# Mask comparisons as differences on GpSimd and signs on ScalarE, rounded query rows copied by a transfer, and reciprocals one unit behind their addition

## The chip, the cores and the metric

One core of one Trainium2 chip runs the kernel. The metric is the device time of one execution in microseconds. Before the change three runs gave a median of 675.91 us (671.8 to 677.35).

## What is computed

The reference is clustered attention followed by two feed-forward blocks, all in float32:

```
# attention: B=2, H=8, S=768, D=64, 16 clusters for each head
q_assign = argmax(normalised q . normalised centroids)      # one of 16 for each query
k_assign = argmax(normalised k . normalised centroids)
mask     = q_assign[..., :, None] == k_assign[..., None, :]
scores   = where(mask, q @ k.T / sqrt(D), -1e9)
attn     = softmax(scores) @ v
# first block: 1536 tokens, 512 -> 2048 -> 512, a rational function between the products
# second block: 512 -> 1024 -> 512, h * softmax(h), a layer norm, then the product
```

The first of equal maxima counts in the argmax.

## The kernel before

**Attention units.** A unit is one head n (16 of them, two batches of 8) and one tile t of 128 queries (6 of them): 96 units. `unit_scores` (L384, L390) makes 128x768 scores in PSUM with four products; there are two such PSUM buffers. Queries and keys are split into rounded parts and remainders, so that the products run in the faster float format: `q1` holds rounded q in rows 0 to 63 and the remainder of q in rows 64 to 127, `q2` holds rounded q again in rows 0 to 63 and 16 rows of the cluster mask behind them; `k1` and `k2` likewise. `unit_max` takes the minimum of the negated scores on VectorE (L395), `unit_exp` the exponential on ScalarE (L408), which also sums a row into `rs`. For every second unit `turn_p` transposes the exponentials on VectorE (L425), and `pv_step` multiplies them with v on TensorE (L435) one head later.

**Heads.** `prep_head(n + 1)` runs in seven steps beside the units of head n, on GpSimd: it rounds k (through `rnd`, L339), takes the remainder of k (L353), rounds q into `q1` and `q2` (both L339), takes the remainder of q (L358) and starts the transfers of the 16 mask rows (L362, L363) on SP's queue. `load_head` (L193, L194) and `load_v` (L202) load later heads on the same queue.

**Masks.** Heads are assigned in five sets. Sets 2, 3 and 4 (two pairs of heads each, q and k) run beside the units, from units 8, 27 and 50; `TCH` says for each step how many units behind that it is placed. `two_sims` and `keep` bring the similarities to the centroids, `to_token` transposes them on VectorE (L302), `top` takes the maximum of each group of 16 (L306), `is_top` compares with it (L310), `rank` multiplies the hits with 16, 15, ..., 1 on GpSimd (L285), `top` and `is_top` again leave only the first hit, `from_token` transposes back (L313), and `mask_out` (L320) scales the result to 0 or a huge number for q and 0 or 1 for k.

**Sums.** For each pair of heads `pair_sums` adds a tiny number to the sums on ScalarE (L460) and takes the reciprocal on VectorE (L461), in the unit t = 0 of the next even head; `sums_out` transposes them two units later on TensorE (L475), sends them through DRAM (L481, L484), and `pair_fin` multiplies with them on GpSimd (L496, L510).

**Order.** The framework orders each engine's instructions by when they are ready in its own model of the program, earlier code first among those that are ready; an engine then runs its queue in that order. `issue_after` and `behind` put an instruction behind another in the queue of its engine. The steps of the masks are queued behind the minimum of their unit on VectorE. Weight conversions for the first block (`w1_f32`: L135 and L138 on ScalarE, L142 on VectorE; `to_parts`: L146, L147) are spread over units 28 to 94. Behind attention come the first block (`ff_h` L745, `ff_y` L797) and the second (`t_h` L873, `t_out` L924).

Of the kernel before, what the change touches and what calls it, by code (L numbers as in the profile page):

```python
# [7 lines left out]
F32 = mybir.dt.float32  # L8
F32R = mybir.dt.float32r
BF16 = mybir.dt.bfloat16  # L10
AF = mybir.ActivationFunctionType
# [5 lines left out]
C = 16  # L17
# [13 lines left out]
def fused_kernel(ctx: ExitStack, tc: tile.TileContext, qT, kT, v, cent, w1, w2i, w2o, gln, coef, centT, cst, out):  # L31
# [20 lines left out]
    def psum1(name):  # L52
# [14 lines left out]
    identb = const.tile([128, 128], BF16, name="identb")  # L67
    nc.gpsimd.tensor_copy(identb, ident)
    rev = cst_t[:, 128:128 + C]
    big = const.tile([128, 1], F32, name="big")  # L70
    nc.vector.memset(big, BIG)
    less = const.tile([128, 1], F32, name="less")
# [17 lines left out]
    S1B = 2  # L90
    AT = (0, 0, 8, 27, 50)
    TCH = {
# [3 lines left out]
    }  # L96

    OLAG = 2
# [141 lines left out]
    def scales(k):  # L240
        es = sets[k]
        m = sm.tile([128, 3], F32, name=f"msc{k}", tag="msc", bufs=2)
        for j, (pp, i) in enumerate(es):
            nc.gpsimd.memset(m[32 * j:32 * j + 32, 0:1], 1.0 if i else -BIG)
            nc.gpsimd.memset(m[32 * j:32 * j + 32, 1:2], 0.0 if i else BIG)
            p = pp % 4
            (nc.vector if k < 1 else nc.gpsimd).tensor_copy(m[32 * j:32 * j + 32, 2:3], cnr[32 * p:32 * p + 32])
        OH[k] = qk.tile([128, S], F32R, name=f"oh{k}", tag="oh", bufs=2)
        for j, (pp, i) in enumerate(es):
            for h in range(2):  # L250
                mk[2 * pp + h, i] = OH[k][32 * j + 16 * h:32 * j + 16 * h + 16]
        MS[k] = m
# [29 lines left out]
    def rank(k, eng):  # L282
        g = 2 * len(sets[k]) * NT
        ev = E[k][1].rearrange("p t (g c) -> p (t g) c", c=C)
        eng.tensor_tensor(ev, ev, rev[:, None, :].to_broadcast([128, g, C]), op=ALU.mult)  # L285
# [19 lines left out]
        tops[k] = sm.tile([128, 48], F32, name=f"my{k}", tag="my48", bufs=2)  # L305
        nc.vector.tensor_reduce(tops[k], E[k][1].rearrange("p t (g c) -> p (t g) c", c=C), axis=AX.X, op=ALU.max)  # L306

    def is_top(k):
        ev = E[k][1].rearrange("p t (g c) -> p (t g) c", c=C)
        nc.vector.tensor_tensor(ev, ev, tops[k][:, :, None].to_broadcast([128, 48, C]), op=ALU.is_equal)  # L310

    def from_token(k):
        nc.vector.transpose(E[k][0], E[k][1].rearrange("p t c -> p (t c)"))  # L313
# [3 lines left out]
    def mask_out(k, o, t):  # L317
        masked[k] += o.shape[-1] * (o.shape[1] if len(o.shape) > 2 else 1)
        M = t.shape[0]
        nc.scalar.activation(out=o, in_=t, func=AF.Identity, scale=MS[k][0:M, 0:1], bias=MS[k][0:M, 1:2])  # L320
# [13 lines left out]
    def rnd(eng, o, a, scale=1.0):  # L334
        if eng is nc.scalar:
            eng.activation(out=o, in_=a, func=AF.Copy, scale=scale)
            return
        if eng is nc.gpsimd:
            eng.tensor_scalar(o, a, scale, 0.0, op0=ALU.mult, op1=ALU.add)  # L339
        elif isinstance(scale, float) and scale == 1.0:  # L340
            eng.tensor_copy(o, a)
        else:
            eng.tensor_scalar(o, a, scale, None, op0=ALU.mult)

    def prep_head(n, er=None, es=None):
        er = er or nc.gpsimd
        es = es or nc.gpsimd
        b, h = divmod(n, H)
        i = n % NB
        a, c = raw.pop(("d", n, 0)), raw.pop(("d", n, 1))  # L350
        rnd(er, k1[i], c, sgn[:, 1:2])
        yield
        es.tensor_tensor(k2[i][0:64], c[0:64], k1[i][0:64].bitcast(F32), op=ALU.subtract)  # L353
        yield
        rnd(er, q1[i], a, sgn[:, 0:1])
        rnd(er, q2[i][0:64], a[0:64], -0.125)
        yield
        es.tensor_tensor(q1[i][64:128], a[64:128], q1[i][64:128].bitcast(F32), op=ALU.subtract)  # L358
        yield
        if n:  # L360
            assert masked[next(k for k, es in enumerate(sets) if (n // 2, 0) in es)] == S
            nc.sync.dma_start(out=q2[i][64:80].bitcast(F32), in_=mk.pop((n, 0)).bitcast(F32))  # L362
            nc.sync.dma_start(out=k2[i][64:80].bitcast(F32), in_=mk.pop((n, 1)).bitcast(F32))  # L363
        yield
# [92 lines left out]
    def pair_sums(key):  # L457

        r = rs.pop(key)
        nc.scalar.activation(out=r, in_=r, func=AF.Identity, bias=tiny)  # L460
        nc.vector.reciprocal(r, r)  # L461
        if key < 7:
            return r

        rw = fin.tile([128, S], F32, name="rw", tag="rb", bufs=1)
        nc.vector.tensor_copy(rw.rearrange("p (t j d) -> p j t d", t=NT, j=2), r[:, :, :, None].to_broadcast([128, 2, NT, D]))
        rb = psum2("s", "rbp")
        for t in range(NT):
            nc.tensor.transpose(rb[:, t // 3, t % 3 * 128:t % 3 * 128 + 128], rw[:, t * 128:t * 128 + 128], ident)
        rsd[key] = rb  # L470

    def sums_out(key, r, u):

        def turned(sp):
            return nc.tensor.transpose(sp[0:12, 0, 384:512], r.rearrange("p j t -> p (j t)"), ident)  # L475

        def spread_out(sp):
            rt = sm.tile([12, 128], F32, name=f"rt{key}", tag="rt", bufs=2)
            nc.scalar.activation(out=rt, in_=sp[0:12, 0, 384:512], func=AF.Copy)
            d = dram.tile([2, S], F32, name=f"rd{key}", tag="rd")  # L480
            nc.sync.dma_start(out=d.rearrange("j (t p) -> (j t) p", p=128), in_=rt)  # L481
            rb = fin.tile([128, S], F32, name=f"rb{key}", tag="rb", bufs=1)
            for j in range(2):
                nc.sync.dma_start(out=rb[64 * j:64 * j + 64], in_=d[j:j + 1, :].to_broadcast([64, S]))  # L484
            rsd[key] = rb

        while u in pre:
            u += 1
        pre[u], post_ = [turned], post.setdefault(u, [])
        post_.append(spread_out)  # L490
# [45 lines left out]
    def assign(k, u, tch):  # L536

        def hook(d, u, f):
            d.setdefault(u, []).append(f)

        def two_sims(c):
            def g(sp):
                for t in range(2):
                    r = sims(k, 2 * c + t, 1, sp[:, t, 384:512])
                return r
            return g

        hook(post, u + tch[0], lambda sp: scales(k))
        for c in range(3):
            hook(pre, u + tch[c], two_sims(c))  # L550
            hook(post, u + tch[c], lambda sp, c=c: keep(k, 2 * c, 2, sp[:, :, 384:512]))
        steps = (to_token, top, is_top, lambda k: rank(k, nc.gpsimd), top, is_top, from_token, lambda k: mask_out(k, OH[k], E[k][0]))
        for i, f in enumerate(steps):
            hook(post, u + tch[3 + i], lambda sp, f=f: f(k))

# [80 lines left out]
    def pv_part(n, t):  # L636
# [4 lines left out]
            return n - 1, c[t - 3], c[t - 2]  # L641
        return (n - 2, (7, 10)[t], (10, 12)[t]) if t < 2 else (-1, 0, 0)

    units = [(n, t) for n in range(B * H) for t in range(NT)]
    NS = S // 64
    for idx, (n, t) in enumerate(units):
# [21 lines left out]
        if m_ >= 0:  # L668
            for i in range(i0, i1):
                pv_step(m_, i)  # L670
        if t == 0 and n and n % 2 == 0:
            sums_out(n // 2 - 1, pair_sums(n // 2 - 1), idx + 2)
        unit_exp(n, t, sp, m)
        if n >= 2 and t in (1, 2):
            pv_out(n - 2, t - 1)
# [345 lines left out]
```

## Time and profile before

| | before |
|---|---|
| median of 3 runs | 675.91 us |
| the profiled execution | 673.62 us |
| its span, first to last instruction | 671.8 us |
| mean granted TensorE clock, share of 2.4 GHz | 0.972 |
| TensorE products busy | 609.3 us (91%) |
| VectorE busy | 495.5 us (74%) |
| ScalarE busy | 437.6 us (65%) |
| GpSimd busy | 391.6 us (58%) |
| moved by DMA | 64.71 MB |

PE is TensorE's products and PEld its weight loads, DVE is VectorE, ACT ScalarE, POOL GpSimd and SP the engine that issues most transfers. A busy share is an average over stages with different limits. Attention fills the span up to about 235 us, the first block follows up to about 500 us, the second to the end.

### The profile page before, as it was taken

To read this page: it belongs to the slowest core of one execution; us is meant where nothing else is said; L and a number is where in the kernel's file an instruction comes from. 1 tells how busy PE (TensorE), PEld (TensorE's weight loads), DVE (VectorE), ACT (ScalarE), POOL (GpSimd) and SP (SyncE) were. 2 spreads that over 40 slices of the span, in tenths; PEclk is the share of its full clock that TensorE was granted. 3 is DMA by queue.
4 is the path that set the end of the run, shared out by engine and by line. 5 is a ranking of instruction groups with operands and counts; after the bars stand their busy time and mean duration, and the time that the engine had idled before them with its cause. 6 is when DMAs were issued, how large, how long until landed. Compare 5 with 4: busy or idle time off the path is not lost.

```text
span 671.8 us, 13803 instructions
## 1 busy us (share of the span) xinstructions
PE 609.3 (91%) x5517; PEld 471.8 (70%) x5517; DVE 495.5 (74%) x648; ACT 437.6 (65%) x796; POOL 391.6 (58%) x363
## 2 busy tenths in 40 slices
PE   7697978888878768999999999999998999999998
PEld 3465655555555556788788777788886888888887
DVE  4789999999999738888977588867689464544360
ACT  2456656765787649989878898786676344434341
POOL 7455667656889338999869899976788000000000
PEclk8589899998999989999999999999998999999999
DMA  8955687777663222323103433300100000000001
GB/s 226 272 180 159 151 224 179 186 193 187 168 182 95 56 96 94 126 95 125 64 0 112 134 111 116 93 1 0 33 0 1 0 1 32 16 32 16 32 17 47
DMA packets 22439, 64.71 MB, mean 96 GB/s; under 512 B 4532, under 2 KB 5640, under 8 KB 22376
## 3 DMA queue, kind: packets, MB, share of 16 engines
q1 hardware_dynamic: 21944, 63.67, 33.4%
q8 instruction: 43, 0.70, 0.4%
q10 hardware_dynamic: 432, 0.17, 0.1%
q14 instruction: 20, 0.16, 0.1%
HBM read 59.16 MB, written 3.19 MB: 93 GB/s over the span
## 4 chain that ended last, share of the span: by engine, by line
PE 42%; POOL 8%; ACT 6%; DVE 3%; issue 2%; DMA 2%; ACTq 0%; POOLq 0%; DVEq 0%
PE y L797 11%; PE hh L873 10%; PE o L924 10%; PE h L745 10%; POOL q L761 2%; POOL gl L780 2%; PE lt L906 2%; POOL q L760 1%; DMA rawv<-in_w2i 1%; POOL vl L147 1%; POOL w1l L147 1%; ACT t L758 1%; ACT h L769 1%; ACT y L759 1%; DVE w1w L142 1%
## 5 line engine op out<-in xcount | busy, mean ns | idle before, releaser
L745 PE MATMUL h<-xhl,w1h 128*128 128x512 f32 x384 | 121.8, 393 | 5.0 <-DVE y L774 3.2
L408 ACT ACTIVATE p<-s,m 128x768 f32<-128x768 f32 x96 | 86.0, 897 | 58.1 <-DVE m L395 57.9
L395 DVE TENSOR_REDUCE m<-s 128x1 f32<-128x768 f32 x96 | 88.4, 933 | 15.8 <-PE s L390 15.4
L435 PE MATMUL pv<-pt,v 32*64 32x192 f32 x3072 | 84.3, 338 | 9.7 <-ACT w L451 6.1
L745 PEld LDWEIGHTS h<-xhl,w1h 128*128 128x128 f32 x384 | 71.7, 188 | 22.5 <-DVE y L774 4.7
L425 DVE STREAM_TRANSPOSE pt<-p 128x1536 f32<-128x1536 f32 x48 | 84.4, 1761 | 0.0
L384 PE MATMUL s<-k,q 128*128 128x384 f32 x192 | 62.5, 410 | 21.9 <-ACT p L408 21.1
L797 PE MATMUL y<-gl,w1h 128*128 128x512 f32 x192 | 76.5, 398 | 5.7 <-POOL gl L780 5.7
L435 PEld LDWEIGHTS pv<-pt,v 32*64 32x64 f32 x3072 | 57.2, 134 | 30.5 <-issue 16.1
L797 PE MATMUL y<-gh,w1l 128*128 128x512 f32 x192 | 76.1, 396 | 0.0
L745 PE MATMUL h<-xhl,w1l 128*128 128x512 f32 x192 | 75.4, 393 | 0.0
L780 POOL TENSOR_TENSOR gl<-y,gh 128x512 fp32r<-128x512 f32 x48 | 66.4, 1384 | 11.5 <-ACT gh L779 11.4
L797 PE MATMUL y<-gh,w1h 128*128 128x512 f32 x192 | 69.6, 394 | 0.1
L761 POOL TENSOR_TENSOR q<-q,t 128x512 f32<-128x512 f32 x48 | 65.3, 1360 | 3.1
L384 PEld LDWEIGHTS s<-k,q 128*128 128x128 f32 x192 | 31.1, 202 | 49.3 <-ACT p L408 27.7
L760 POOL TENSOR_SCALAR q<-t,ab 128x512 f32<-128x512 f32 x48 | 41.9, 873 | 29.7 <-ACT t L758 20.3
L762 DVE TENSOR_TENSOR y<-y,h 128x512 f32<-128x512 f32 x48 | 32.8, 683 | 32.3 <-ACT y L759 32.1
L390 PE MATMUL s<-k,q 128*128 128x384 f32 x192 | 52.4, 356 | 2.3 <-DVE k L595 2.3
L873 PE MATMUL hh<-vh,xhl 128*128 128x512 f32 x192 | 53.9, 395 | 0.0
L797 PEld LDWEIGHTS y<-gl,w1h 128*128 128x128 f32 x192 | 36.3, 189 | 17.0 <-POOL gl L780 9.1
L797 PEld LDWEIGHTS y<-gh,w1h 128*128 128x128 f32 x192 | 36.1, 189 | 8.6 <-ACT gh L779 0.5
L797 PEld LDWEIGHTS y<-gh,w1l 128*128 128x128 f32 x192 | 36.3, 189 | 8.0
(151 smaller groups left out, 1330.5 us busy)
## 6 DMA issues: line engine op xcount, KB each, us to landing
raww<-in_w SPq DMA_DIRECT2D x32, 512.0 KB, 4.5
v<-in_v SPq DMA_DIRECT2D x64, 192.0 KB, 4.6
dup<-in_qT SPq DMA_DIRECT2D x31, 192.0 KB, 4.1
dup<-in_kT SPq DMA_DIRECT2D x31, 192.0 KB, 3.8
rawv<-in_w2i SPq DMA_DIRECT2D x8, 512.0 KB, 3.5
rawv<-in_w2o SPq DMA_DIRECT2D x8, 512.0 KB, 3.5
out<-ob SPq DMA_DIRECT2D x11, 256.0 KB, 2.0
pr<-in_qT SPq DMA_DIRECT2D x7, 384.0 KB, 4.0
```

Of the source, the lines that this page charges most:

```text
L384: r = nc.tensor.matmul(sp[:, a, 0:384], lhsT=q1[i][:, sl], rhs=k1[i][:, a * 384:(a + 1) * 384], start=True, stop=False)
L390: last["pe"] = nc.tensor.matmul(sp[:, a, 0:384], lhsT=q2[i][:, sl], rhs=k2[i][:, a * 384:(a + 1) * 384], start=False, stop=True)
L395: last["dve"] = nc.vector.tensor_reduce(m, sp[:, :, 0:384], axis=AX.XY, op=ALU.min)
L408: last["act"] = nc.scalar.activation(out=P[n, t // 2][:, t % 2], in_=sp[:, :, 0:384], func=AF.Exp, scale=-1.0, bias=m, accum_out=rs[key][: ...
L425: r = nc.vector.transpose(PT[n][:, 2 * i:2 * i + 2].rearrange("p t k -> p (t k)"), p.rearrange("p t a k -> p (t a k)"))
L435: last["pv"] = nc.tensor.matmul(pv[n][64 * c:64 * c + 64, r, 0:192].rearrange("p (t q) -> p t q", t=NT), lhsT=vv[n][sl, j], rhs=PT[n][sl, ...
L745: r = nc.tensor.matmul(hp, lhsT=w[:, kt * 128:(kt + 1) * 128], rhs=x[:, kt], start=(i == 0), stop=(i == 11))
L761: nc.gpsimd.tensor_tensor(q, q, t, op=ALU.mult)
L780: nc.gpsimd.tensor_tensor(gl, y, gh.bitcast(F32), op=ALU.subtract)
L797: nc.tensor.matmul(o, lhsT=w[:, c], rhs=g, start=(first and i == 0), stop=(last and i == 2))
L873: last["th"] = nc.tensor.matmul(hp[:, a], lhsT=y[:, kt], rhs=w[:, 512 * a:512 * a + 512], start=(kt == 0 and e == 0), stop=(kt == 3 and e ...
L924: r = nc.tensor.matmul(op[:, 0:m], lhsT=l[:, kt], rhs=w, start=(n == 0), stop=(n == 23))
```

## The change

In sets 2, 3 and 4 the two comparisons become a difference to the maximum on GpSimd (`below`) and its sign on ScalarE (`hot`): 0 at the maximum, -1 elsewhere. The rank step becomes an addition of 16/32, 15/32, ... on GpSimd (`rank_at`), after which only the first hit is the maximum. `mask_out` has another offset to fit. Two steps are added, so `TCH` is written anew; the second maximum comes earlier in it than before. In `prep_head` rows 0 to 63 of `q2` are no longer rounded on GpSimd but copied from `q1` by a transfer on SP's queue. `sums_out` is called one unit later than `pair_sums`, and the reciprocal of the first seven pairs moves into it, queued on VectorE behind the minimum of that unit.

```
+    rev_n = const.tile([128, C], F32, name="revn")
+    nc.vector.tensor_scalar(rev_n, rev, 2.0 ** -5, None, op0=ALU.mult)
...
-        2: (0, 1, 2, 3, 4, 5, 6, 10, 11, 12, 13),
-        3: (0, 1, 2, 3, 5, 6, 7, 12, 13, 14, 15),
-        4: (0, 1, 2, 3, 5, 6, 7, 12, 13, 14, 15),
+        2: (0, 1, 2, 3, 4, 4, 5, 6, 9, 9, 11, 12, 13),
+        3: (0, 1, 2, 3, 5, 5, 6, 7, 10, 10, 13, 14, 15),
+        4: (0, 1, 2, 3, 5, 5, 6, 7, 10, 10, 13, 14, 15),
...
-            nc.gpsimd.memset(m[32 * j:32 * j + 32, 1:2], 0.0 if i else BIG)
+            nc.gpsimd.memset(m[32 * j:32 * j + 32, 1:2], (0.0 if i else BIG) if k < 2 else float(i))
...
-    def is_top(k):
+    def below(k):
         ev = E[k][1].rearrange("p t (g c) -> p (t g) c", c=C)
-        nc.vector.tensor_tensor(ev, ev, tops[k][:, :, None].to_broadcast([128, 48, C]), op=ALU.is_equal)
+        nc.gpsimd.tensor_tensor(ev, ev, tops[k][:, :, None].to_broadcast([128, 48, C]), op=ALU.subtract)
+
+    def rank_at(k):
+        ev = E[k][1].rearrange("p t (g c) -> p (t g) c", c=C)
+        nc.gpsimd.tensor_tensor(ev, ev, rev_n[:, None, :].to_broadcast([128, 48, C]), op=ALU.add)
+
+    def hot(k):
+        ev = E[k][1].rearrange("p t c -> p (t c)")
+        nc.scalar.activation(out=ev, in_=ev, func=AF.Sign)
...
         rnd(er, q1[i], a, sgn[:, 0:1])
-        rnd(er, q2[i][0:64], a[0:64], -0.125)
+        nc.sync.dma_start(out=q2[i][0:64].bitcast(F32), in_=q1[i][0:64].bitcast(F32))
...
-        nc.vector.reciprocal(r, r)
         if key < 7:
             return r
+        nc.vector.reciprocal(r, r)
...
+        behind(nc.vector.reciprocal(r, r), last["dve"])
         while u in pre:
...
-        steps = (to_token, top, is_top, lambda k: rank(k, nc.gpsimd), top, is_top, from_token, lambda k: mask_out(k, OH[k], E[k][0]))
+        steps = (to_token, top, below, hot, rank_at, top, below, hot, from_token, lambda k: mask_out(k, OH[k], E[k][0]))
...
+    due = []
...
-        if t == 0 and n and n % 2 == 0:
-            sums_out(n // 2 - 1, pair_sums(n // 2 - 1), idx + 2)
+        if t < 2 and n and n % 2 == 0:
+            if t:
+                sums_out(n // 2 - 1, due.pop(), idx + 2)
+            else:
+                due.append(pair_sums(n // 2 - 1))
```

## Rows read from the trace of the kernel before

**Rows 1.** Busy time of engines in four stretches: span, then engines, clock, DMA.

```profile
core 0: us, PE busy (x) PEld busy (x) DVE busy (x) ACT busy (x) POOL busy (x), PEclk, DMA share, GB/s
45.00:230.00 185.00, 153.01 (x3157) 106.83 (x3161) 171.94 (x161) 128.41 (x250) 128.46 (x111) 0.98 0.64 169
250.00:500.00 250.00, 243.76 (x1049) 195.84 (x1048) 199.69 (x277) 210.17 (x355) 211.96 (x175) 1.00 0.24 76
63.00:72.00 9.00, 6.90 (x109) 4.64 (x110) 9.00 (x9) 5.85 (x11) 6.54 (x15) 0.81 0.73 181
146.00:157.00 11.00, 7.76 (x135) 5.07 (x141) 10.33 (x9) 6.11 (x13) 8.95 (x8) 0.84 0.86 219
```

**Rows 2.** Groups of instructions by form, 45 to 230 us.

```profile
line engine op names shapes xcount | busy us, mean ns | idle before us <-releasers
L395 DVE TENSOR_REDUCE m<-s 128x1 f32<-128x768 f32 x84 | 77.2, 932 | 8.0 <-PE s L390 7.6
...
L425 DVE STREAM_TRANSPOSE pt<-p 128x1536 f32<-128x1536 f32 x42 | 73.9, 1761 | 0.0
...
L339 POOL TENSOR_SCALAR q<-dup 64x768 fp32r<-64x768 f32 x13 | 11.5, 884 | 0.0
...
L142 DVE SCALAR_TENSOR_TENSOR w1f<-w1f,raww 128x512 uint32<-128x512 uint32 x10 | 9.8, 976 | 0.0
...
L310 DVE TENSOR_TENSOR e<-e,my 128x768 f32<-128x768 f32 x6 | 8.3, 1381 | 0.0
...
L285 POOL TENSOR_TENSOR e<-e,cst 128x768 f32<-128x768 f32 x3 | 5.8, 1939 | 3.7 <-DVE e L310 3.7
...
L320 ACT ACTIVATE oh<-sm,msc 128x768 fp32r<-128x768 f32 x3 | 3.0, 1016 | 0.0
```

**Rows 3.** Waits, 45 to 230 us, then SP's of the whole span: total, times, longest.

```profile
ACT p L408 <- DVE m L395: 49.5, 43, 2.6
...
PE s L384 <- ACT p L408: 17.1, 25, 1.7
...
DVE m L395 <- PE s L390: 7.6, 10, 1.3
...
DVE rs L461 <- ACT rs L460: 5.3, 5, 1.4
...
SPq L193 <- POOL k L353: 27.3, 8, 4.2
```

**Rows 4.** VectorE in order of time: start, duration, instruction, idle before.

```profile
147.57 2.22 DVE L310 TENSOR_TENSOR e<-e,my 128x768 f32<-128x768 f32 x1
149.71 0.68 DVE L142 SCALAR_TENSOR_TENSOR w1f<-w1f,raww 128x512 uint32<-128x512 uint32 x1
...
166.41 0.92 DVE L310 TENSOR_TENSOR e<-e,my 128x768 f32<-128x768 f32 x1
```

**Rows 5.** TensorE in order of time, behind the first and the sixth comparison.

```profile
52.59 0.62 PE L384 MATMUL s<-k,q 128*128 128x384 f32 x2 [0.73 <-ACT p L408]
...
169.43 0.59 PE L384 MATMUL s<-k,q 128*128 128x384 f32 x2 [1.42 <-ACT p L408]
```

**Rows 6.** VectorE and TensorE in order of time around one reciprocal.

```profile
129.61 0.23 DVE L461 RECIPROCAL rs<-rs 128x12 f32<-128x12 f32 x1 [0.82 <-ACT rs L460]
129.75 1.75 DVE L395 TENSOR_REDUCE m<-s 128x1 f32<-128x768 f32 x2
...
129.79 0.51 PE L390 MATMUL s<-k,q 128*128 128x384 f32 x2
```

**Rows 7.** GpSimd in order of time, beside the comparison at 147.57.

```profile
147.16 1.81 POOL L496 TENSOR_TENSOR u<-u,w 128x768 f32<-128x768 f32 x1 [2.05 <-ACT w L451]
```

**Rows 8.** Head 7's rounding, its first scores, and transfers with KB and landing.

```profile
102.07 0.91 POOL L339 TENSOR_SCALAR q<-dup,sgn 128x768 fp32r<-128x768 f32 x1
...
114.15 0.59 PE L384 MATMUL s<-k,q 128*128 128x384 f32 x2 [0.94 <-ACT p L408]
...
dup<-in_kT SPq DMA_DIRECT2D x31, 192.0 KB, 3.8
```

**Rows 9.** VectorE and GpSimd in order of time at the start.

```profile
5.46 0.15 DVE L226 TENSOR_SCALAR cnr<-cnr 128x1 f32<-128x1 f32 x1 [4.09 <-POOL cnr L225]
...
8.23 0.60 POOL L68 CAST identb<-cst 128x128 bf16<-128x128 f32 x1
```

## The prediction

> **What bounds the kernel now.** I read the windows first [rows 1]. From 45 to 230 us the attention units run, 84 of the 96. VectorE is busy 171.9 of 185 us there, TensorE 153.0, ScalarE 128.4 and GpSimd 128.5. From 250 to 500 us, in the feed-forward part, TensorE is busy 243.8 of 250. So attention is paced by VectorE with TensorE close behind, and the rest by TensorE. Whatever attention ends earlier, the whole kernel ends earlier, because the part behind it has nothing else to wait for.
>
> The table of groups [rows 2] says what VectorE does: the minimum of a unit (0.932 us each) and the transpose of two units (1.761 us) are 151.1 us of the 172. The reader is to see that what is left is small and that the mask comparisons (L310) are its second largest item: 6 instructions, 8.3 us, 1.381 us each.
>
> The waits [rows 3] confirm the order: the exponential on ScalarE waits 49.5 us for the minimum on VectorE, and TensorE's scores wait 17.1 us for an exponential that must free their PSUM buffer (there are two). VectorE itself waits only 7.6 us for scores and 5.3 us, 5 times, for the addition ahead of the reciprocal (L461).
>
> A unit costs 185/84 = 2.20 us. Two numbers are enough to see how tight the ring is: VectorE needs (77.2 + 73.9)/84 = 1.80 us for each unit, TensorE 153.0/84 = 1.82 us. Time that leaves VectorE comes out at the end only where TensorE then stands idle and can start earlier.
>
> **The change part by part.**
>
> **Comparisons off VectorE.** Six instructions go. They took between 0.92 us (at 166.41) and 2.22 us (at 147.57), and the next instruction starts 0.08 us before the listed end (149.71 against 147.57 + 2.22 = 149.79) [rows 4]. With that overlap for each, 8.3 - 0.5 = 7.8 us leave the queue. Does TensorE wait behind them? Behind the first it sits idle 0.73 us, behind the sixth 1.42 us, each time for an exponential, and there is such a gap of 0.7 to 1.7 us behind all six [rows 5]. So I take all of it: **-7.8**, with -3.9 as the poor end, if half of each gap only becomes a wait for scores.
>
> **TensorE's clock.** Around two of the long comparisons the granted clock was 0.81 (9 us) and 0.84 (11 us) of the 2.4 GHz level, while it was 0.98 over the stage [rows 1]: TensorE had stood idle just before. That is 9 x 0.19 + 11 x 0.16 = 3.5 us of lost clock. Some of it was idle time anyhow. I take **-1.0**, between 0 and -3.5.
>
> **Reciprocals one unit later.** The five waits of 5.3 us go [rows 3]. What is late next? At 129.61 VectorE waited 0.82 us; the two minima behind it then ran back to back from 129.75 [rows 6]. Without the wait the first could start at once. The second needs scores that TensorE finished only at 130.30 and would start there instead of at about 130.6. So of 0.82 us about 0.3 is gained directly; the first exponential, and with it the next scores, comes some 0.8 us sooner, which the transposes partly hide. 0.4 us for each of five is **-2.0**, between 0 and -5.3. The transposition of the sums on TensorE follows two units behind, so nothing waits for the moved reciprocal.
>
> **Signs on ScalarE.** Six 128x768 activations from SBUF to SBUF are added; the same form, the mask's last step (L320), takes 1.016 us [rows 2]. ScalarE has 49.5 us of waiting in 43 places [rows 3], so most fit. One that stands ahead of an exponential whose minimum is ready delays it by up to 1.0 us. Behind a minimum there is 0.93 + 1.76 = 2.7 us of VectorE work before the next-but-one minimum, while exponential and scores need some 2.1 us, so about half a us of such a delay is free. I take **+1.5** for all six, between 0 and +6.1.
>
> **Differences on GpSimd.** Six 128x768 subtractions are added; the rank multiplication becomes an addition of the same form (L285, 1.939 us) [rows 2]: 6 x 1.94 = 11.6 us more. The rounded copies of q leave: 13 in the stage of 0.884 us each = 11.5 us less. GpSimd is idle 57 us in the stage [rows 1], so its own time costs nothing. What counts is who waits for it. VectorE's second maximum now waits for a chain subtraction, sign, addition of 1.94 + 1.02 + 1.94 = 4.9 us, and its last transposition for 1.94 + 1.02 = 3.0 us. The unit numbers leave 5 units for the first chain (4 to 9, 5 to 10), some 11 us, and 3 or 4 units for the second, at least 6.6 us. Queued on VectorE behind a late one are the next minimum and hence the exponential. Between no wait and six waits of the size of the reciprocals' (5.3/5 = 1.06 us each, 6.4) I take **+1.2**, nearest to none, because of these distances.
>
> **Both engines at one port.** At 147.57 the comparison took 2.22 us, not 0.92, while a GpSimd addition ran from 147.16 to 148.97 [rows 4, 7]: VectorE's own 0.92 us began only when GpSimd had ended. The weight conversions (L142, 10 of them, 0.976 us on average against the 0.68 of the one at 149.71) remain and have two inputs in SBUF too [rows 2, 4]. GpSimd holds 11.6 us more in long pieces and 11.5 us less in short ones, so I take **+0.5**, between 0 and +5.8 (half of 1.94 us for each new piece).
> The Trainium skill's page "SBUF — State Buffer", section "Who interferes with whom", says that a VectorE instruction with two SBUF inputs and a GpSimd instruction that reads SBUF exclude each other for a whole instruction. By that rule, the trace agrees at 147.57, and the moved comparisons would come to hold against VectorE what they used to suffer.
>
> **Copies of q by transfer.** 15 transfers of 192 KB, on SP's queue, replace 15 GpSimd steps. Each waits for the rounding of q. For head 7 that ended at 102.98 and its first scores started at 114.15 [rows 8], 11.2 us later; a transfer of this size, a key half, lands in 3.8 us [rows 8], and the masks' transfers go into the same tile behind it in any case. SP already waits 27.3 us for GpSimd's key remainder ahead of the next loads [rows 3], so what is queued behind the new transfer (next head's q, k and v) is not the late one. If that cover were gone, a head would start 3.8 us late. **0**, up to +1.
>
> **A constant at the start.** One 128x16 product on VectorE, about the 0.15 us of L226; if it stands ahead of L226 and its input lands only when GpSimd reads it (8.23 us), it costs 8.23 - 5.46 = 2.8 us [rows 9]. **+0.1**, between 0 and 2.8, as it can be queued later.
>
> **The sum**: -7.8 - 1.0 - 2.0 + 1.5 + 1.2 + 0.5 + 0 + 0.1 = **-7.5 us**. The profiled execution took 673.6 us (span 671.8 and 1.8 us around it) and would take 666.1. The median of the runs shown, 675.9, lies 2.3 us above it; against that the forecast is **668.4 us**, 1.1% less.
>
> **The rivals.**
>
> *Signs hold up the exponentials (slower).* ScalarE works in order. If the sign of a unit is queued ahead of the next exponential, that one waits for the subtraction and the sign: 1.94 + 1.02 = 3.0 us behind the maximum, while its own minimum is ready 0.9 us behind it, so 2.1 us late; 4.0 us if GpSimd first ends another long product. Six times 3.0 is 18 us against the 10.8 gained: +7.2, about **683**. It decides from 1.8 us a piece (10.8/6). For it: sets 3 and 4 give the first sign one unit, 2.2 us, less than these 3.0. Against it: a queue's order is not the code's. GpSimd ran the second remainder for head 3 ahead of set 2's rank step, which comes earlier in the code and was not ready; a sign may be put behind an exponential in the same way.
>
> *TensorE takes over.* At 1.82 us a unit it needs as much as VectorE. Half of the comparisons (-3.9), 0.3 us for each reciprocal (-1.5), costs as above (+3.3): -2.1, about **674**. For it: the minima waited for scores 10 times even now. Against it: TensorE's idle gaps stand just behind the comparisons.
>
> *Everything comes through.* -7.8 - 3.5 - 5.3 and no more than 1.6 of costs: -15, **661**.
>
> *The port.* The forecast plus the bound of the port, 5.3 us more: **674**. This is what the skill's rule above would do if each new piece met a VectorE instruction with two inputs; there are only 10 such, and their mean of 0.976 us says that a few are met now.
>
> **How the numbers follow.** Chances: forecast 0.52, signs 0.12, TensorE 0.22, everything 0.10, port 0.04. Under 1%, about 6.8 us, this kernel's measurement hardly tells from no change. The forecast lies at that edge, on its far side in some 7 of 10 of its cases. Faster by over 1%: 0.10 + 0.36 + 0.03 = 0.49; within: 0.39; slower: 0.12. The range runs from 660 (everything) to 678 (the milder half of the signs' case) and leaves out 2 in 10.
>
> **What would show it.** Right: no L310 on VectorE, its busy time in the stage some 8 to 10 us less, no wait of VectorE for the addition of the sums, the windows at 63 and 146 us at clock 0.95 or more, feed-forward starting 7 us earlier. Wrong: ScalarE waiting for GpSimd ahead of a sign, VectorE waiting for GpSimd ahead of the second maximum, TensorE's scores waiting for the transfer of q, or the minima waiting for scores by as much as the comparisons cost.

## The result and the profile after

The changed kernel takes 683.29 us (median of 4 runs, 680.84 to 687.6) against 675.47 us for the kernel before: ratio 1.0123, 95% interval 1.0081 to 1.0165. The forecast was 668.4 us with a range up to 678. The time is that of the rival in which signs hold up the exponentials, which gave 683 us and had a chance of 0.12.

The profiled execution took 687.6 us (before: 673.62). It is the slowest of the four, 4.3 us above the median, so its waits are read for their kind and place more than for their sum. Lines have moved in the changed kernel: scores are L394 and L400, the minimum L405, the exponential L418; of the masks' steps, the maximum is L308, the difference L312, the rank addition L316 and the sign L320.

The windows come first (columns as in [rows 1]):

```profile
core 0: us, PE busy (x) PEld busy (x) DVE busy (x) ACT busy (x) POOL busy (x), PEclk, DMA share, GB/s
45.00:230.00 185.00, 148.95 (x2927) 104.43 (x2918) 152.55 (x146) 123.71 (x239) 119.45 (x99) 0.92 0.68 177
250.00:500.00 250.00, 239.46 (x1197) 193.11 (x1198) 189.79 (x265) 202.74 (x344) 206.15 (x168) 0.99 0.25 81
100.00:120.00 20.00, 9.02 (x173) 6.22 (x157) 14.67 (x15) 7.28 (x15) 12.47 (x9) 0.86 0.49 137
120.00:140.00 20.00, 16.54 (x296) 11.45 (x297) 12.68 (x12) 13.71 (x25) 8.98 (x7) 0.80 0.72 193
```

VectorE is busy 152.6 us of the stage where it was busy 171.9 [rows 1]. The forecast wanted 8 to 10 us less, and at first sight 19 us less looks like success. But the other engines are less busy too, and the granted clock is 0.92 instead of 0.98: nobody has taken over as the bound, all of them stand still at times. Between 100 and 120 us TensorE works 9 of 20 us, and the 20 us behind it run at 0.80 of the 2.4 GHz level.

The groups by form, 45 to 230 us, show that the edit itself did what it says: no comparison is left on VectorE, six differences stand on GpSimd and six signs on ScalarE.

```profile
line engine op names shapes xcount | busy us, mean ns | idle before us <-releasers
L405 DVE TENSOR_REDUCE m<-s 128x1 f32<-128x768 f32 x78 | 72.4, 935 | 28.9 <-PE s L400 28.7
...
L144 DVE SCALAR_TENSOR_TENSOR w1f<-w1f,raww 128x512 uint32<-128x512 uint32 x10 | 9.1, 906 | 0.0
...
L312 POOL TENSOR_TENSOR e<-e,my 128x768 f32<-128x768 f32 x6 | 9.4, 1571 | 1.3 <-DVE my L308 1.0
...
L320 ACT ACTIVATE e<-e 128x768 f32<-128x768 f32 x6 | 5.0, 840 | 19.7 <-POOL e L312 19.7
```

78 units' minima fit into the 185 us where 84 did [rows 2]: 2.37 us a unit instead of 2.20. Both new pieces are cheaper than assumed (1.57 us for a difference, not 1.94; 0.84 us for a sign, not 1.02). What they cost is in the last column of L320: 19.7 us in which ScalarE stood ahead of a sign. The waits of the same stretch (total, times, longest):

```profile
ACT p L418 <- DVE m L405: 34.8, 30, 2.4
DVE m L405 <- PE s L400: 28.7, 21, 5.8
...
ACT e L320 <- POOL e L312: 19.7, 5, 9.9
...
PE s L485 <- DVE rs L497: 8.1, 3, 5.7
POOL xf L521 <- DMA rb<-rd: 7.1, 1, 7.1
...
DVE my L308 <- POOL e L316: 3.5, 1, 3.5
```

Against [rows 3]: the exponential waits 14.7 us less for its minimum, since some of that time is now spent in front of a sign; the minimum waits 28.7 us for scores instead of 7.6; in the stretch shown next, the scores wait for exponentials that a sign held up. The wait for the addition ahead of the reciprocal (L461) is gone, and besides the signs' wait the last three of the list are new.

One such wait, in order of time (start, duration, engine, instruction, idle before):

```profile
61.17 0.91 POOL L349 TENSOR_SCALAR k<-dup,sgn 128x768 fp32r<-128x768 f32 x1 [5.21 <-PE s L394]
62.05 0.91 POOL L349 TENSOR_SCALAR q<-dup,sgn 128x768 fp32r<-128x768 f32 x1
...
64.82 1.83 POOL L368 TENSOR_TENSOR q<-dup,q 64x768 fp32r<-64x768 f32 x1
66.72 1.49 POOL L312 TENSOR_TENSOR e<-e,my 128x768 f32<-128x768 f32 x1
...
68.25 0.84 ACT L320 ACTIVATE e<-e 128x768 f32<-128x768 f32 x1 [4.81 <-POOL e L312]
69.00 0.88 ACT L418 ACTIVATE p<-s,m 128x768 f32<-128x768 f32 x1
...
70.02 1.01 PE L394 MATMUL s<-k,q 128*128 128x384 f32 x2 [3.65 <-ACT p L418]
...
62.33 0.94 DVE L308 TENSOR_REDUCE my<-e 128x48 f32<-128x768 f32 x1
...
64.88 1.79 DVE L405 TENSOR_REDUCE m<-s 128x1 f32<-128x768 f32 x2
...
71.71 0.96 DVE L405 TENSOR_REDUCE m<-s 128x1 f32<-128x768 f32 x1 [3.36 <-PE s L400]
```

The maximum is ready at 63.27. GpSimd has four preparation steps of the next head ahead of the difference, from 61.17 to 66.72, so the difference runs 3.4 us late. ScalarE waits 4.81 us for it with the sign first in its queue. Two minima were done at about 65.8 and 66.67; their exponentials start only at 69.00. TensorE idles 3.65 us for them, comes back slower (1.01 us for a pair of products that takes 0.62 in [rows 5]), and VectorE idles 3.36 us. Scores, minimum and exponential follow each other in a ring over two PSUM buffers; one sign out of place stops all of it.

The longest one, 9.94 us, has another cause in front of it:

```profile
108.55 1.96 POOL L521 TENSOR_TENSOR xf<-u,rb 128x512 f32<-128x512 f32 x2 [7.07 <-DMA rb<-rd]
110.47 1.80 POOL L316 TENSOR_TENSOR e<-e,revn 128x768 f32<-128x768 f32 x1
...
112.30 0.95 DVE L308 TENSOR_REDUCE my<-e 128x48 f32<-128x768 f32 x1 [3.54 <-POOL e L316]
...
115.19 0.37 PE L485 MATMUL s<-cst,rs 128*12 128x128 f32 x1 [5.68 <-DVE rs L497]
...
118.19 1.49 POOL L312 TENSOR_TENSOR e<-e,my 128x768 f32<-128x768 f32 x1
...
119.72 0.84 ACT L320 ACTIVATE e<-e 128x768 f32<-128x768 f32 x1 [9.94 <-POOL e L312]
```

`sums_out` of the second pair is one unit later, and then finds the units in which set 3's similarities stand, so its products start at 90.79 instead of 77.65. Its result goes through DRAM and comes back too late for GpSimd's multiplication L521, the rank addition is queued behind that, VectorE's second maximum waits for the addition, the next reciprocal stands behind the maximum, and the next sums on TensorE wait for the reciprocal. The two moved parts of the change are chained here. The four preparation steps of a head stand ahead of the difference here too: the second maximum is ready at 113.25, and the difference starts at 118.19.

The five waits of signs are 1.51, 4.81, 9.94, 1.43 and 2.06 us. Three are hardly more than the difference itself lasts; the two followed above make up 14.8 of the 19.7.

The first product of the feed-forward part starts at 261.44 us, where it was 246.84, 14.6 us later; from there to the end both kernels need 425 us (424.4 and 425.0). All of the loss is in attention.

### The profile page after: what moved, and what is told of

It reads as the page before. It is cut to its first block, busy times and chain, and to the rows that moved or that the text cites. A ratio compares the mean times of both kernels' runs of the same rounds, so it can differ in the third digit from the quotient of the medians.

```text
span 685.8 us, 13862 instructions
## 1 busy us (share of the span) xinstructions
PE 616.3 (90%) x5517; PEld 478.5 (70%) x5517; DVE 486.7 (71%) x643; ACT 441.7 (64%) x802; POOL 388.4 (57%) x354
## 4 chain that ended last, share of the span: by engine, by line
PE 39%; POOL 9%; ACT 6%; DVE 3%; issue 3%; DMA 2%; ACTq 0%; POOLq 0%; DVEq 0%
PE y L812 10%; PE hh L888 10%; PE o L939 10%; PE h L760 8%; POOL q L776 2%; POOL gl L795 2%; POOL w1l L149 2%; POOL q L775 2%; PE lt L921 2%; POOL vl L149 1%; DMA rawv<-in_w2i 1%; ACT t L773 1%; DVE w1w L144 1%; ACT h L784 1%; ACT y L774 1%
## 5 line engine op out<-in xcount | busy, mean ns | idle before, releaser
L405 DVE TENSOR_REDUCE m<-s 128x1 f32<-128x768 f32 x96 | 89.2, 937 | 39.4 <-PE s L400 39.2
L418 ACT ACTIVATE p<-s,m 128x768 f32<-128x768 f32 x96 | 85.9, 896 | 47.1 <-DVE m L405 46.4
L445 PE MATMUL pv<-pt,v 32*64 32x192 f32 x3072 | 88.1, 352 | 13.4 <-ACT w L461 12.7
L445 PEld LDWEIGHTS pv<-pt,v 32*64 32x64 f32 x3072 | 59.5, 140 | 35.6 <-ACT w L461 18.0
L394 PE MATMUL s<-k,q 128*128 128x384 f32 x192 | 65.2, 424 | 15.4 <-ACT p L418 14.5
L795 POOL TENSOR_TENSOR gl<-y,gh 128x512 fp32r<-128x512 f32 x48 | 67.1, 1398 | 11.0 <-ACT gh L794 10.8
L394 PEld LDWEIGHTS s<-k,q 128*128 128x128 f32 x192 | 32.6, 211 | 43.0 <-ACT p L418 21.2
L400 PE MATMUL s<-k,q 128*128 128x384 f32 x192 | 55.4, 374 | 2.3 <-DVE k L606 2.3
L349 POOL TENSOR_SCALAR k<-dup,sgn 128x768 fp32r<-128x768 f32 x15 | 13.6, 905 | 50.3 <-PE s L394 22.8
```

What stands on the lines that cost most here:

```text
L394: r = nc.tensor.matmul(sp[:, a, 0:384], lhsT=q1[i][:, sl], rhs=k1[i][:, a * 384:(a + 1) * 384], start=True, stop=False)
L405: last["dve"] = nc.vector.tensor_reduce(m, sp[:, :, 0:384], axis=AX.XY, op=ALU.min)
L418: last["act"] = nc.scalar.activation(out=P[n, t // 2][:, t % 2], in_=sp[:, :, 0:384], func=AF.Exp, scale=-1.0, bias=m, accum_out=rs[key][: ...
L445: last["pv"] = nc.tensor.matmul(pv[n][64 * c:64 * c + 64, r, 0:192].rearrange("p (t q) -> p t q", t=NT), lhsT=vv[n][sl, j], rhs=PT[n][sl, ...
L795: nc.gpsimd.tensor_tensor(gl, y, gh.bitcast(F32), op=ALU.subtract)
```

## The experiments

All ran five rounds beside the kernel before, whose median there was 674.3 to 674.8 us; differences in us are the ratio times 674.4. Where a run needs a part of the diff above alone, it is named and not shown again.

### Each part by itself: a_only, b_only, c_only, c_same_unit

**a_only** has the differences, signs, new offsets and `TCH`, and neither the transfers nor the moved reciprocals.

> Only the comparisons are moved; rounding and reciprocals stay as before. First theory (a sign waits in ScalarE's queue for a subtraction that GpSimd has queued behind the next head's rounding): slower than before by 4 to 10 us, 680 to 686 us, ScalarE waiting for GpSimd ahead of signs by 10 to 20 us in all. Second theory (the sums come four units late for the second pair, GpSimd waits for them and everything behind it): the larger part of the loss is gone, 670 to 677 us. Third theory (the transfer of q makes heads start late): not slower than before, 668 to 675 us.

683.13 us, ratio 1.0117 (1.0091 to 1.0143): +7.9 us. Signs wait 14.4 us, 5 times, 5.6 at the longest. The comparisons' part alone is as slow as the whole.

**b_only** has the transfer of q alone.

> Only rows 0 to 63 of q2 are copied by a transfer. First and second theory: within 3 us of before, 672 to 679 us, no wait of TensorE's scores for the transfer. Third theory: slower by 4 us or more, with scores waiting for the copy or loads landing later.

670.12 us, ratio 0.9928 (0.9903 to 0.9953): -4.9 us, where the forecast had 0. Window and groups of its stage:

```profile
45.00:230.00 185.00, 152.82 (x3210) 106.87 (x3216) 170.29 (x162) 129.30 (x252) 118.81 (x98) 1.00 0.73 183
...
L142 DVE SCALAR_TENSOR_TENSOR w1f<-w1f,raww 128x512 uint32<-128x512 uint32 x10 | 8.3, 830 | 0.0
L310 DVE TENSOR_TENSOR e<-e,my 128x768 f32<-128x768 f32 x6 | 7.5, 1254 | 0.0
```

GpSimd is busy 9.7 us less, and the two groups of VectorE with two inputs in SBUF take 15.8 us instead of 18.1 [rows 2] although nothing of theirs was edited: 2.3 us of collisions are gone, and the clock is 1.00. One can be followed: in the kernel before, the comparison at 64.01 took 1.69 us, as GpSimd's remainder of q ran until 64.89; with one rounding step fewer ahead of it that remainder ends at 64.25, and the comparison at 64.19 takes 0.94. The trace doesn't show the whole gain: in the two profiled executions the feed-forward part starts only 1.1 us earlier (245.71 against 246.84).

The comparison before, then GpSimd's remainder and the comparison in b_only:

```profile
64.01 1.69 DVE L310 TENSOR_TENSOR e<-e,my 128x768 f32<-128x768 f32 x1
```

```profile
62.42 1.83 POOL L358 TENSOR_TENSOR q<-dup,q 64x768 fp32r<-64x768 f32 x1
...
64.19 0.94 DVE L310 TENSOR_TENSOR e<-e,my 128x768 f32<-128x768 f32 x1
```

**c_only** has the reciprocals and `sums_out` as in the change; **c_same_unit** moves the reciprocal alone and leaves the sums' products in their old unit:

```
-                sums_out(n // 2 - 1, due.pop(), idx + 2)
+                sums_out(n // 2 - 1, due.pop(), idx + 1)
```

> Only the reciprocals and the transposition of the sums come one unit later. First and third theory: the five waits of VectorE (5.3 us) are gone and 0 to 3 us are gained, 672 to 676 us; the sums of the second pair come four units later, but no one waits for them without the moved comparisons. Second theory: slower by 2 us or more, GpSimd waiting for the sums from DRAM.

> As c_only, but the sums are transposed in the unit of before (one unit behind the reciprocal, not two), so that they don't give way to the similarities of set 3. First theory: as c_only within 2 us. Second theory: 2 to 5 us faster than c_only. If the reciprocal is then too close to its transposition, TensorE waits for it by some 0.5 us each, 7 times.

c_only 673.78 us, ratio 0.9984 (0.996 to 1.0008); c_same_unit 681.27, 1.0103 (1.0072 to 1.0134), 7 to 8 us slower than c_only, where the expectation had it within 2 us or faster. VectorE's five waits went in both, and came back elsewhere. Waits of c_only, then of c_same_unit:

```profile
PE s L475 <- DVE rs L487: 7.2, 5, 2.5
POOL xf L511 <- DMA rb<-rd: 5.0, 2, 4.7
```

```profile
PE s L475 <- DVE rs L487: 14.4, 6, 3.9
```

The reciprocal was 0.2 us long and 1.06 us late on VectorE. Moved behind the next minimum, it is late for TensorE, which waits 1.4 us each time even with the sums one unit later, 2.4 us without.

### Where a sign stands: a_hold, a_first, a_dve

**a_hold** is a_only with each sign queued behind the exponential of the unit before its own. By its trace it moves three of the six, the second signs of sets 2, 3 and 4, by one, two and two exponentials (18, 38 and 61 exponentials stood ahead of them in a_only, 19, 40 and 63 here):

```
-        nc.scalar.activation(out=ev, in_=ev, func=AF.Sign)
+        behind(nc.scalar.activation(out=ev, in_=ev, func=AF.Sign), last["act"])
```

> As a_only, but each sign is queued on ScalarE behind the exponential before its own unit; this moves two of the six signs, the second ones of sets 2 and 3, behind one more and two more exponentials. First theory: the two longest waits for GpSimd become short or fall beside idle time, 4 to 6 us are won back, 676 to 680 us. Rival (signs cost by themselves): as a_only, 682 to 684 us.

676.29 us, 1.0024 (0.9996 to 1.0053): 6.3 us of the 7.9 come back by the place of three signs (the expectation had two). Signs still wait 5.8 us, 3 times.

**a_first** is a_only with the difference queued ahead of the rounding on GpSimd, and three heads prepared two units later to make room:

```
+    def later(r):
+        if "sub" in last:
+            behind(r, last["sub"])
...
-        rnd(er, k1[i], c, sgn[:, 1:2])
+        later(rnd(er, k1[i], c, sgn[:, 1:2]))
...
-                spread(prep_head(n + 1), 7, idx, idx + 6)
+                spread(prep_head(n + 1), 7, idx + (2 if n in (5, 6, 9) else 0), idx + 6)
```

> As a_only, but GpSimd's queue holds each subtraction ahead of the next head's rounding instead of behind it (three heads' rounding starts two units later for that); ScalarE's queue is the same. First theory (the wait is GpSimd's place for the subtraction): the signs' waits fall from 14 us to under 5, VectorE's missing comparisons now count, 668 to 674 us. Rival (signs on ScalarE and long products on GpSimd cost by themselves, wherever they stand): as a_only, 680 us or more. Rival (the rounding comes too late for its head): the signs wait little, but scores wait for the rounding.

692.17 us, 1.025 (1.02 to 1.03), the slowest of all, where the first theory had 668 to 674. Its waits, 45 to 230 us:

```profile
POOL e L312 <- DVE my L308: 34.8, 5, 12.5
...
ACT e L320 <- POOL e L312: 7.4, 5, 1.5
PE s L398 <- POOL q L372: 7.2, 1, 7.2
PE s L404 <- DMA k<-oh: 5.5, 1, 5.5
```

The signs wait no more than the difference lasts, 1.5 us each. But now GpSimd stands up to 12.5 us ahead of a difference whose maximum is not there yet, with the next head's rounding behind it, and TensorE waits 7.2 us for a rounded q and 5.5 for mask rows. The wait can be moved between queues; it doesn't go away.

**a_dve** is a_only with the difference on VectorE (`nc.vector` for `nc.gpsimd`).

> As a_only, but the six differences are taken on VectorE, which costs it what the comparisons cost before; signs stay on ScalarE and the rank addition on GpSimd. First theory: signs follow VectorE closely and wait little, so only their own 0.84 us each can cost: 673 to 679 us. Rival (the signs' own time on ScalarE is the loss): 680 us or more.

684.68 us, 1.0134 (1.0084 to 1.0184), no better than a_only, and outside the 673 to 679 of the first theory. The profiled execution is the fastest of six (676.46 us):

```profile
ACT e L320 <- DVE e L312: 12.1, 6, 3.0
```

A sign waits for its difference with VectorE as the producer too, six times of six, and the time is lost without a difference on GpSimd. How much of a_only's loss GpSimd's queue adds is not separated here, as a_dve also puts the six differences back on VectorE. By itself this run would also fit the rival that the signs' own time is the loss; a_hold, which has all six signs, and ab_hold2_nosign below speak against that.

### What the transfer of q costs: b_none

**b_none** writes rows 0 to 63 of `q2` for the first two heads only, with no transfer:

```
-        rnd(er, q2[i][0:64], a[0:64], -0.125)
+        if n < NB:
+            rnd(er, q2[i][0:64], a[0:64], -0.125)
```

> Rows 0 to 63 of q2 are written for the first two heads only and neither rounded nor copied after that (the scores of later heads lose a part of the computation). If b_only's gain of 4.8 us comes from GpSimd's missing steps, this gains as much, 668 to 672 us. If the transfers cost something too, it gains 1 to 3 us more than b_only. If the gain came from something that the transfer does, it is as before, 674 us.

670.64 us, 0.9952 (0.9921 to 0.9983), not to be told from b_only. The 15 transfers (192 KB, landing in 3.3 us) cost nothing that shows; the gain is the steps' absence from GpSimd.

### Putting parts together: ab, after_hold, ab_hold2, b_clate

**ab** is the change without the moved reciprocals, **after_hold** the whole change with the line of a_hold. **ab_hold2** is ab with that line, and with first signs one unit later (for set 2 also the second maximum a unit earlier). **b_clate** is b_only with the reciprocals moved and the sums three units behind.

```
-        2: (0, 1, 2, 3, 4, 4, 5, 6, 9, 9, 11, 12, 13),
-        3: (0, 1, 2, 3, 5, 5, 6, 7, 10, 10, 13, 14, 15),
+        2: (0, 1, 2, 3, 4, 4, 6, 6, 8, 8, 11, 12, 13),
+        3: (0, 1, 2, 3, 5, 5, 7, 7, 10, 10, 13, 14, 15),
```

> The whole change without the moved reciprocals. If the parts add up (a_only +8.4, b_only -4.7 us), 678 to 680 us, and the moved reciprocals then cost the whole change some 4 us, by the sums that come four units late for the second pair and hold up GpSimd's queue ahead of the rank addition. If the reciprocals are neutral there too, as in c_only, this is as the whole change, 682 to 684 us.

> The whole change with each sign queued behind the exponential before its own unit. If only the signs' places decide, it wins back what a_hold won, 8 us: 673 to 677 us. If the late sums hold up GpSimd and VectorE's second maximum by themselves, less: 677 to 681 us, with VectorE waiting for the rank addition and TensorE for the reciprocal as before.

> Comparisons moved and q copied, the first sign of each set one unit later as well, all signs behind the exponential before their unit, reciprocals as before. First theory (the signs' waits were the loss): signs wait under 3 us in all, and with b_only's gain 664 to 671 us, faster than before and than b_only. If the signs or the long GpSimd products cost by themselves: 672 to 676 us.

> q copied; reciprocals one unit later, and the sums transposed three units behind them instead of two, so that TensorE does not stand waiting for the reciprocal (7.2 us in c_only). If that wait was what took c_only's gain: 3 to 5 us below b_only, 665 to 668 us. If VectorE's five waits were hidden anyhow: as b_only, 669 to 671 us.

| kernel | us | ratio, 95% interval |
|---|---|---|
| ab | 680.81 | 1.007 (1.0038 to 1.0102) |
| after_hold | 675.78 | 1.0008 (0.9975 to 1.0041) |
| ab_hold2 | 671.33 | 0.9934 (0.9901 to 0.9966) |
| b_clate | 673.39 | 0.9964 (0.993 to 0.9997) |

In the whole change the place of the signs is worth 1.0123 - 1.0008, 7.8 us. In ab the longest wait of a sign is 4.8 us and neither GpSimd's multiplication with the sums nor the second maximum waits: the 9.94 us chain belongs to the moved reciprocals together with the differences. In after_hold, which has both, the first links are there again:

```profile
PE s L485 <- DVE rs L497: 7.6, 4, 3.9
POOL xf L521 <- DMA rb<-rd: 5.9, 2, 5.3
...
ACT e L320 <- POOL e L312: 5.0, 4, 1.5
```

In b_clate TensorE no longer waits for a reciprocal, but GpSimd's multiplication (L511 there) waits 8.9 us for the sums, and the kernel is no faster than b_only: the moved reciprocals bring nothing that can be measured in either place.

In ab_hold2 no sign waits at all. That should have shown the -7.8 us of the comparisons on top of b_only's gain, and it is level with b_only. The last experiments are about that.

### What the comparisons were worth: cmp_none, bcmp_none, ab_hold2_nosign, ab_hold3

**cmp_none** is the kernel before, **bcmp_none** b_only, with the comparisons taken out of the list of steps and every other step where it was; **ab_hold2_nosign** is ab_hold2 without its signs; **ab_hold3** is ab_hold2 with set 2 one unit earlier.

```
-        steps = (to_token, top, is_top, lambda k: rank(k, nc.gpsimd), top, is_top, from_token, ...)
+        steps = (to_token, top, lambda k: None, lambda k: rank(k, nc.gpsimd), top, lambda k: None, from_token, ...)
...
-    AT = (0, 0, 8, 27, 50)
+    AT = (0, 0, 7, 27, 50)
```

> The kernel before with the six mask comparisons on VectorE left out (part of the assignment is thus not computed), every other step where it was: the ceiling of what moving them away can bring. The sum's first term says -7.8 for the queue and -1.0 for the clock, so about 666 against 674.5. The theory that VectorE's time is not what ends the units there (the next scores come as late as before) says 0 to -2, so 672 to 674.5.

> The query rows copied by transfer (670.1 by itself) and the six comparisons left out. If the copies' gain is made of the same collisions of VectorE with GpSimd as the comparisons' gain, the two don't add: 666 to 668. If they are separate they add to about 662.

> The held variant with first signs one unit later (671.3), its six signs left out, differences on GpSimd kept (the assignment is not fully computed). If the signs' own 0.84 us each and their place between exponentials ate the comparisons' gain, it comes to 663 to 665. If the differences on GpSimd or the late mask of set 2 ate it, it stays at 669 to 672.

> The held variant with set 2 started one unit earlier. There the scores of head 4 waited 3.2 us for the mask rows, and VectorE 3.4 us for the scores, at a clock of 0.83 afterwards. If the late mask is what ate the gain, the wait goes and the time falls by 3.5 to 5, to about 667. If the gain was lost in many small places, it stays at 670 to 672.

| kernel | us | ratio, 95% interval |
|---|---|---|
| cmp_none | 668.98 | 0.9943 (0.9915 to 0.9972) |
| bcmp_none | 667.72 | 0.9893 (0.9866 to 0.9921) |
| ab_hold2_nosign | 672.02 | 0.9968 (0.9946 to 0.9989) |
| ab_hold3 | 670.27 | 0.9909 (0.9876 to 0.9942) |

Deleting the comparisons, with nothing in their place, brings 3.8 us (1.9 to 5.7), half of the first term, between what the two theories said. Its stage shows where the other half went. SP's queue, TensorE and VectorE in order of time, then a group:

```profile
69.87 1.02 SPq L363 DMA_DIRECT2D k<-oh  x1
...
75.16 0.59 PE L390 MATMUL s<-k,q 128*128 128x384 f32 x2 [1.93 <-DMA k<-oh]
...
75.79 0.96 DVE L395 TENSOR_REDUCE m<-s 128x1 f32<-128x768 f32 x1 [1.72 <-PE s L390]
79.29 0.96 DVE L395 TENSOR_REDUCE m<-s 128x1 f32<-128x768 f32 x1 [2.55 <-PE s L390]
```

```profile
L142 DVE SCALAR_TENSOR_TENSOR w1f<-w1f,raww 128x512 uint32<-128x512 uint32 x10 | 10.9, 1093 | 0.0
```

TensorE stands 1.93 us within head 4's first scores, for mask rows that SP issued at 69.87, behind four transfers of v; behind that wait the granted clock from 72 to 85 us is 0.87. The first two minima of head 4 wait 1.72 and 2.55 us for scores, where in the kernel before the same two waited 0 and 0.55. The other minima together wait 1.3 us less than before. The stage has become shorter up to here, and runs into mask rows that had been in time before. Counted over the same units, from the 13th minimum (at 48.89 us before and 50.32 here) to the feed-forward part, VectorE waits 2.4 us more for scores (11.5 against 9.1), and the conversions take 1.1 us more (10.9 against 9.8 in [rows 2]): the one at 147.53 now meets the GpSimd addition that a comparison met before. 8.3 us of comparisons, less 0.5 of overlap, less 2.4, less 1.1, leaves 4.3; the stretch is 4.0 us shorter (193.92 against 197.95).

On top of b_only the comparisons are worth 2.4 us by the medians (0.9928 - 0.9893); the intervals don't tell that from 3.8. Here, too, TensorE waits 2.0 us for head 4's mask rows.

Without its signs ab_hold2 is no faster: six signs of 0.84 us that wait for nothing cost nothing that shows within intervals of about 2 us either way. What remains in ab_hold2 is the same late mask. TensorE, then SP's queue of ab_hold2:

```profile
78.18 0.98 PE L400 MATMUL s<-k,q 128*128 128x384 f32 x2 [3.21 <-DMA k<-oh]
...
69.36 1.96 SPq L204 DMA_DIRECT2D v<-in_v  x4
...
72.79 0.59 SPq L373 DMA_DIRECT2D k<-oh  x1
```

The mask rows of set 2 are issued behind four transfers of v and land when head 4 should have begun; VectorE then stood 3.39 us, and the clock from 65 to 85 us was 0.83. In ab_hold3 the mask is ready one place sooner and its transfer stands ahead of v:

```profile
68.07 0.59 SPq L373 DMA_DIRECT2D k<-oh  x1
68.76 1.92 SPq L204 DMA_DIRECT2D v<-in_v  x4
```

That wait is gone and the clock of the same 20 us is 0.91, in an execution that is the fastest of its twelve (665.58 us). The median, 1.1 us lower, can't be told from ab_hold2 by the intervals, so what the late mask costs in a typical execution stays open. ab_hold3 and b_only both beat the kernels before and after; which of the two is the better is left open.

## Why the prediction was wrong

**What bounds the kernel** was right: the loss is all in attention, and every us lost there came out at the end.

**Signs on ScalarE** (+1.5, up to +6.1) is the term that failed, and with it the dismissal of the rival. The step was "a queue's order is not the code's ... a sign may be put behind an exponential in the same way". It was not: a sign stood where ScalarE had to wait for it in 5 of 6 cases. The rival had forecast 18 us of waiting in six pieces of 3.0; there were 19.7 in five, three of 1.4 to 2.1, one of 4.8 and one of 9.9. That the sums agree is luck, and so in part is the 683: the rival set 10.8 us of gains against its waits, of which the runs show 3.8 (cmp_none) and 1.1 (c_only), and it had nothing of the 4.9 that the copies of q bring. Its mechanism was right, its cause only in part: behind the long waits is a difference that stands behind four preparation steps of a head (5.5 us), and in one case behind L521. a_hold and after_hold show it by experiment, 6.3 and 7.8 us for the place of three signs. The signs' own time, on which the +1.5 was built, costs nothing that shows (ab_hold2_nosign).

**Comparisons off VectorE** (-7.8). "So I take all of it" was too much: deleting them brings 3.8 us, the size of the term's poor end (-3.9), but not for its reason. That end, and the rival "TensorE takes over", had half of every gap become a wait for scores. In the trace of cmp_none the waits for scores grew at two minima alone, by 3.7 us, behind the late mask rows of head 4, and nowhere else. The prediction asked whether the copies of q arrive in time and never asked it of the mask rows. The gaps of [rows 5] hold but for the comparison at 64.01: the exponential's gap behind it is 0.45 us, and the longer one, 1.51, is for a transposition.

**The clock** (-1.0). The two windows at 63 and 146 us have 1.00 in cmp_none, as forecast. But they have 1.00 in b_only too, where the comparison at 146.79 still takes 2.22 us, so a long comparison doesn't bring the clock down by itself; and cmp_none falls to 0.87 in another place, behind the mask wait. In the changed kernel the stage fell to 0.92; its stretch at 0.80 (120 to 140 us) follows TensorE's idle times of 5.68 and 5.28 us.

**Reciprocals** (-2.0): alone -1.1 us, between -2.7 and +0.5. "Nothing waits for the moved reciprocal" was wrong: TensorE waited for it five times (7.2 us) and GpSimd for the later sums. In the change this also made the longest sign wait. Its share there, 1.0123 against ab's 1.007, is 3.6 us by the medians, but the intervals overlap.

**Differences on GpSimd** (+1.2). GpSimd's time was no issue and VectorE waited for an addition only once, 3.5 us. What was late was the difference, in GpSimd's own queue; the prediction counted units of distance and named the queue behind VectorE, not the one in front of the difference. On price, the Trainium skill's "GPSIMD Engine Reference", section "Engine selection", puts a two-input elementwise step at about twice VectorE's time. Here 1.57 us stand against 0.92 us for the comparison at 166.41 [rows 4], 1.7 times; the difference itself takes 0.91 us on VectorE in a_dve where it is shortest.

**The port** (+0.5) and **copies of q** (0, up to +1). The new GpSimd pieces did not make VectorE's conversions longer: 0.906 us on average against 0.976. The cover of the copies was read rightly: no scores wait for the transfer, and b_none is no faster. But the working asked only what the transfer adds, and took GpSimd's removed 11.5 us as worth nothing because GpSimd had idle time. b_only is 4.9 us faster (3.2 to 6.5). 2.3 us of this are read off as collisions with VectorE; the rest is not settled, and whether the better clock is part of it is not shown. The Trainium skill's "SBUF — State Buffer", section "Who interferes with whom", bears on this: by it a VectorE step with two SBUF inputs contends with a GpSimd step that reads SBUF, for ports that one of them holds alone. The trace agrees (1.69 us at 64.01 became 0.94 where the step beside it ended earlier). The rule cuts both ways: work taken off GpSimd, or ended sooner, can speed up VectorE.

**The constant** (+0.1): 0.72 us on VectorE at 6.56, but the first unit's minimum starts at 19.97 instead of 19.89. No cost shows.

Added up, the parts measured alone give +7.9 - 4.9 - 1.1 = +1.9 us; the whole has +8.3. By the medians 1.7 of the missing 6.4 us come when the copies join the comparisons (ab), and 4.7 when the reciprocals join both, but the intervals are as wide as that. The trace shows one such meeting, the 9.94 us chain; how the rest is divided is open.

## What to carry to other kernels

Before a step is handed to an in-order engine that feeds the bound, write down what stands ahead of its producer and what stands behind the step itself; ahead of a step of 0.84 us ScalarE stood up to 9.9 us here, and moving three of six by one or two places gave most of the loss back. Before work is taken off the bounding engine, run the kernel with that work deleted: here it gave 3.8 of 8.3 us, and its trace named what the shorter stage ran into, mask rows that had been in time before. Work taken off an engine with idle time can still pay: 4.9 us here, of which 2.3 are read off as fewer collisions with the bounding engine.

## What the hardware showed that was not expected

- A difference to a broadcast maximum took 1.49 or 1.50 us on GpSimd in five cases of six, and 1.94 in the one at 99.54, which started beside a weight conversion on VectorE (98.24 to 100.13); an addition of a broadcast row of the same 128x768 takes 1.80 us at the least and 1.94 on average.
- A sign of 128x768 from SBUF to SBUF takes 0.84 us between exponentials, less than the mask's last step, a scaling with an offset, of the same shape but with output in the faster float format (1.02 us).
- 48 KB of mask rows, issued behind four transfers of v, held up TensorE for 3.21 us in ab_hold2 and 1.93 us in cmp_none; issued ahead of them, and 4.7 us sooner, in ab_hold3, they did not.
